# A gated mix of an S4 convolution and a gMLP on one core: the token bias added by VectorE, preparation products taken off GpSimd, idle TensorE work in waits, K products in two groups, and a new order

## The chip, the cores and the metric

The kernel runs on one core of one Trainium2 chip. A core has five engines with instruction streams of their own: TensorE (PE; its weight loads are listed apart as PEld), VectorE (DVE), ScalarE (ACT), GpSimd (POOL) and SyncE (SP), which here only issues DMAs. The metric is the device time of one execution in microseconds, the median of several runs. All operands are bfloat16, accumulation is in float32.

## The reference, cut to what matters

```python
x = A_u                                               # (1, 2048, 640)
g = _sigmoid((x * gate_w).sum(-1, keepdims=True))
a = _A_ref(x, A_re, A_im, B_re, B_im, C_re, C_im, log_dt, Dskip)
b = _B_ref(x, w_in, w_sp, b_sp, w_out)
return g * a + (1 - g) * b

def _A_ref(...):                                      # S4: N = 128 modes per channel
    logdA = dt * A;  dB = dt * Bc
    P = jnp.exp(logdA[:, :, None] * l)                # l = 0 .. 2047
    K = jnp.einsum('dn,dnl,dn->dl', Cc, P, dB).real   # a kernel of 2048 taps per channel
    return irfft(rfft(u padded) * rfft(K padded))[:2048] + u * Dskip

def _B_ref(...):                                      # gMLP, F = 1728, Fh = 864
    z = _gelu(x @ w_in)
    z1 = z[..., :Fh];  z2 = _layernorm(z[..., Fh:])
    g = jnp.einsum('ts,bsf->btf', w_sp, z2) + b_sp[None, :, None]
    return (z1 * g) @ w_out
```

The change touches one term above all: `+ b_sp`, a number for each token t, added to the spatial product before it is multiplied by z1.

## The kernel before, in words

The work is described as tasks, not as a finished program. `add` (L153) notes a task with its engine or a choice of engines, an estimated duration in us, the tiles it reads and writes, and a bias; `dma` (L406) does so for a transfer on a queue of SP or POOL. `Plan.run` (L187) then simulates the engines with these durations, takes for each free engine the ready task with the highest priority (the longest chain behind it, plus its bias), and issues the real instructions in the order found. Where a task names two engines (`("DVE", "ACT")`), the simulation picks one. `TUNE` (L38) adds numbers to the biases, keyed by function, line within the function and a loop index; so the order on every engine is searched offline, and a changed cost or bias moves instructions all over the program. Tiles are taken from rings of a fixed number of buffers (L446); a task that needs a new buffer waits for the last user of the old one.

The stages, in order of time:

- *z2* (`z2_tile`, L587): for each of 16 token tiles ten matmuls of 432 columns (L593), gelu on ACT (L597), a tanh for the gate logit (L599), and sums for the layernorm by DVE (L605) or ACT (L601). A column with gate_w is appended to the weights: it is loaded as `gw5`, transposed on TensorE (L558) and copied by ACT (L560).
- *Preparation* (L728 to L769): products of the S4 parameters on 128 x 640 tiles, by the helpers `ptt` (two tensors, L704), `pts` (scalars, L709), `ftt`/`fts` (with a permuted output, L720/L724) and `pstt`. Most of them may run on DVE or POOL (`pd`). Instructions that these record have the helper's line (L707, L722, L365, L367).
- *z1* (`z1_tile`, L616): 512 tokens by two feature tiles at a time, gelu, and a store to DRAM.
- *Spatial blocks* (`sp_block`, L791): eight blocks of 256 tokens. w_sp arrives transposed (`wT`). For each of seven feature tiles 16 matmuls of 256 columns (L811) accumulate in `ps_g`, two feature tiles to a PSUM tile, and a seventeenth matmul with one contraction row (L813) adds the bias: a row of ones as weights, the bias row `br` (1 x 256) as moving operand. DVE multiplies ps_g by z1 into `vT` (L817, 512 wide; L820, 256 wide on 96 partitions for the last feature tile). Then 28 matmuls with Wout (L834) make `ps_o`, which DVE or ACT scales by 1 - g (L838) into `ob` (stored to DRAM) or, for the last four token tiles, `acc`.
- *K* (`k_exps`, `k_tables`, `k_sub`): in eight steps of 80 channels, exponentials and sines of multiples of the S4 parameters are made by DVE, POOL and ACT into a table ET (two buffers), the multiples among them by `si` (L1003), `ci` and `ai` (L963, L970) and the products by L1019 to L1030. Each step ends in 160 small matmuls (L1047, L1048) in a single task, whose PSUM result goes to `kf` (L1056, L1058) and through DRAM into the layout of the convolution.
- *Convolution*: a factorised Fourier transform, stage 1 of the input (`s1_u`, L640) and of K (`conv_s1`, L1122), the frequency products (`conv_s2`, L1157) with matmuls L1183, L1190, L1198, ACT copies `us` and `vs` and the DVE product `p` (L1192), a DVE transpose (`conv_vt`, L1206), and the inverse (`conv_i2`, L1249) with matmuls L1276/L1278. `i2_out` (L1218) multiplies by g and adds what the gMLP left. The channels are split in a wide part of 480 (h = 0) and a narrow one of 160 (h = 1).

The planned order interleaves the spatial blocks with K and stage 1, so that TensorE has the large products to do while the tables are made.

Of the kernel before, what the change touches and what calls it, by code (L numbers as in the profile page):

```python
# [25 lines left out]
class Handle:  # L26
# [12 lines left out]
    ('conv_s1', 15, ('g', 0)): -4782,  # L39
    ('conv_s2', 35, ('h', 1)): 8481,  # L40
    ('conv_s2', 34, ('h', 0)): 2130,
    ('conv_s2', 34, ('h', 1)): 5372,
    ('conv_s2', 42, ('h', 0)): -1046,
    ('conv_s2', 10, None): 8445,
    ('conv_s2', 14, ('h', 0)): 7450,
    ('conv_s2', 28, None): -242,
    ('conv_vt', 4, ('g', 1)): 16792,
    ('conv_vt', 4, ('g', 2)): 6435,
    ('eights', 6, None): 416,
    ('i2_out', 7, None): -8356,  # L50
    ('k_expand', 28, ('h', 0)): -4317,
    ('k_store', 13, ('h', 0)): 409,
    ('k_sub', 23, None): -4028,
    ('k_sub', 13, ('h', 1)): -5731,
    ('k_tables', 31, ('c', 1)): -9085,
    ('k_tables', 31, None): -2311,
    ('k_tables', 32, None): -5160,
    ('k_tables', 41, ('c', 6)): -7528,
    ('k_tables', 41, None): 3002,
    ('k_tables', 30, None): -7406,  # L60
    ('k_tables', 29, ('c', 2)): -3413,
    ('k_tables', 6, ('c', 2)): 10829,
    ('k_tables', 6, None): -8182,
    ('k_tables', 18, None): 336,
    ('k_tables', 36, ('c', 1)): 8144,
    ('k_tables', 36, None): -161,
    ('k_tables', 20, ('c', 2)): -24903,
    ('k_tables', 20, ('c', 6)): 3906,
    ('k_tables', 20, None): 5307,
    ('k_tables', 21, ('c', 0)): -2613,  # L70
    ('k_tables', 21, ('c', 2)): -28734,
    ('k_tables', 21, None): 7786,
    ('k_tables', 38, ('c', 6)): 11198,
    ('main', 347, None): -1664,
    ('main', 151, ('g', 1)): -2430,
    ('main', 151, ('g', 2)): -4398,
    ('main', 151, ('g', 3)): 29821,
    ('main', 151, None): 1954,
    ('main', 155, None): -1160,
    ('main', 149, None): 906,  # L80
    ('main', 418, None): -10013,
    ('main', 428, None): 7379,
    ('main', 427, None): -8690,
    ('main', 416, None): 58,
    ('quads', 6, None): -16700,
    ('s1_u', 13, ('n0', 2)): 6950,
    ('s1_u', 13, ('n0', 6)): -34683,
    ('s1_u', 16, ('h', 1)): 3532,
    ('s1_u', 16, ('n0', 0)): -364,
    ('s1_u', 16, ('n0', 12)): -37434,  # L90
    ('s1_u', 16, ('n0', 14)): 7826,
    ('s1_u', 16, ('n0', 6)): 3687,
    ('s1_u', 16, None): 3318,
    ('s1_u', 3, ('n0', 12)): 2341,
    ('s1_u', 3, ('n0', 4)): 9125,
    ('s1_u', 18, ('h', 1)): -25774,
    ('s1_u', 18, ('n0', 10)): -2673,
    ('s1_u', 18, ('n0', 4)): -3986,
    ('s1_u', 18, None): -1598,
    ('s1_u', 14, ('h', 1)): -2482,  # L100
    ('s1_u', 14, ('n0', 10)): 4719,
    ('s1_u', 14, ('n0', 4)): -4980,
    ('s1_u', 14, ('n0', 8)): -2369,
    ('s1_u', 14, None): -1332,
    ('sp_block', 28, ('tb', 0)): -5958,
    ('sp_block', 25, ('tb', 6)): 7709,
    ('sp_block', 22, ('tb', 0)): 4394,
    ('sp_block', 22, ('tb', 1)): 1583,
    ('sp_block', 22, ('tb', 6)): -85,
    ('sp_block', 22, ('tb', 7)): 7901,  # L110
    ('sp_block', 44, None): 2232,
    ('sp_block', 45, ('tb', 0)): -19742,
    ('sp_block', 50, ('tb', 2)): -4255,
    ('sp_block', 50, ('tb', 4)): -4889,
    ('sp_block', 50, ('tb', 5)): -664,
    ('sp_block', 50, None): 3599,
    ('sp_block', 3, None): 2228,
    ('sp_block', 8, ('tb', 0)): 27668,
    ('sp_block', 8, None): -3475,
    ('sp_block', 6, None): 11944,  # L120
    ('tg_build', 6, None): 2671,
    ('tg_build', 9, ('c', 0)): 4671,
    ('x_group', 3, ('g', 0)): 2653,
    ('x_group', 3, ('g', 1)): 432,
    ('x_group', 3, ('g', 2)): 3697,
    ('x_group', 3, None): -2901,
    ('z1_tile', 10, ('g', 2)): 850,
    ('z1_tile', 10, None): 4674,
    ('z2_tile', 18, ('h', 0)): -22,
    ('z2_tile', 18, None): -6544,  # L130
# [4 lines left out]
class Plan:  # L135
# [51 lines left out]
    def run(self):  # L187
# [26 lines left out]
        dma = 0.0  # L214
        fset = None
# [7 lines left out]
        while len(order) < N:  # L223
# [10 lines left out]
            while again:  # L234
                again = False
                for e in self.ENG:
# [38 lines left out]
                    for h in t["hs"]:  # L275
                        if h in slot:
                            continue
                        slot[h] = allocs[h.ring]
                        allocs[h.ring] += 1
                        freed[h.ring].append(None)  # L280
                    end = now + max(c - self.OV.get(e, 0.0), 0.03) if c else now
                    if t["nb"]:
                        s = max(end + (0.0 if t["hold"] else 1.0), dma)
                        dma = s + t["nb"] / 1e6
                        fin = dma + (2.5 if t["hold"] else 1.4) + (1.2 if e == "POOL" else 0.0)
                        if t["hold"]:
                            end = dma
                    else:
                        fin = now + c + self.LAT.get(e, 0.0)
# [35 lines left out]
def kernel(  # L325
# [20 lines left out]
    P = 128  # L346
# [57 lines left out]
    QC = {"SP": 0.42, "POOL": 0.6, "ACT": 0.3}  # L404
# [115 lines left out]
    ones = const.tile([1, P], BF, name="ones")  # L520
    vec.memset(ones[:], 1.0)
# [38 lines left out]
    S_(add("ACT", 0.2, lambda e: act.copy(out=Win2[:, :, Fh], in_=psm()[:, 0:ND]), r=[psm], w=["gwt"], bias=9900))  # L560
    add("DVE", 0.3, lambda e: vec.tensor_copy(out=idf[:], in_=ident[:]), r=["pre3"], w=["idf"], bias=1000)
# [142 lines left out]
    def ptt(o, a, b, op, eng=("POOL",)):  # L704
        bf = a in nat or b in nat
# [14 lines left out]
    def ftt(o, a, b, op, eng):  # L720
        cs = [dict(POOL=5.0, DVE=0.3 + dv1(D))[x] for x in eng]
        add(eng, cs, lambda e: parts(e, o, (a, b), lambda o_, i_: E_[e].tensor_tensor(out=o_, in0=i_[0], in1=i_[1], op=op)), r=[a, b, "ptmp"], w=[o], bias=2500)  # L722
# [69 lines left out]
    def sp_block(tb):  # L792
# [6 lines left out]
        br = sbt(lambda: gsp, "br", "br", [1, 256])  # L799
        dma("SP", lambda: br()[:], lambda: brv[:, 256 * tb:256 * tb + 256], 512, r=["br_d"], w=[br], bias=1000 - 100 * tb)  # L800
        vT = []
        for f0 in range(0, NFT, 2):
            ps = gps("ps_g", [P, 2, 256])
            fts = range(f0, min(NFT, f0 + 2))
            for ft in fts:
                fs = fsz[ft]

                for c0 in range(0, NS, 4):
                    def m(e, ft=ft, fs=fs, ps=ps, f0=f0, c0=c0):
                        for st in range(c0, c0 + 4):  # L810
                            pe.matmul(ps()[0:fs, ft - f0, :], lhsT=z2n[:, st, 128 * ft:128 * ft + fs], rhs=wT()[:, st, :], start=(st == 0), stop=False)  # L811
                        if c0 + 4 == NS:
                            pe.matmul(ps()[0:fs, ft - f0, :], lhsT=ones[0:1, 0:fs], rhs=br()[:], start=False, stop=True)  # L813
                    add("PE", (4 + (c0 + 4 == NS)) * mm(256), m, r=([(wT, 0), (wT, 1), br] if c0 == 0 else [wT, br]) + ([(ps, f0)] if ft > f0 and c0 == 0 else []) + [("z2n", s) for s in range(c0, c0 + 4)], w=[(ps, ft)], bias=-1000 - 100 * tb)
            v_ = sbt(lambda: gsp, "vT", "vT", [P, 2, 256], bufs=4)
            if f0 < 6:
# [552 lines left out]
```

## Time and profile before

| | us |
|---|---|
| median of 5 runs | 362.28 (360.02 to 363.6) |
| the profiled execution | 363.6 |
| its span | 361.8 |
| TensorE busy (mean granted clock 0.973) | 325.2 |
| VectorE busy | 280.1 |
| ScalarE busy | 239.3 |
| GpSimd busy | 155.5 |
| 896 spatial matmuls L811, busy | 113.1 |
| 32 + 16 products p (L1192), busy | 47.9 |

Busy time of TensorE counts each matmul from its start to a modelled end, and successive matmuls overlap: 896 x 276 ns would be 247 us, yet the group's busy time is 113.1. What a matmul takes from its engine is therefore read from the starts of its neighbours in the timeline. The clock of TensorE is not constant; the profile gives the granted share for each stretch. A line of the profile's list of groups names the line in the code, the engine, the operation, the written and read tiles, the shape, the count, then the busy time and the mean of one in ns, and after the last bar the idle time of the engine just before them and what ended it. A line of waits reads "engine, tile and line that waited <- engine, tile and line that it waited for: us in total, times, the longest".

### The profile page before, as it was taken

The page shows a single profiled execution, that of the slowest core. Times are in us where ns is not written, and L with a number is a line of the kernel's source. Part 1 is how long each engine was busy: PE and PEld are TensorE (multiplying, and loading weights), DVE is VectorE, ACT ScalarE, POOL GpSimd, SP SyncE. Part 2 cuts the span into 40 slices and gives each one's busy share as a digit, 9 for nine tenths or more (in the row PEclk, how much of TensorE's full clock was granted, in tenths as well). Part 3 has the DMA queues.
Part 4 walks back from the last instruction along what each step waited for, and adds up shares of the span by engine and source line. Part 5 has one row for each costly group of instructions (what it writes and reads, how often), then busy time and mean ns, then how long its engine had stood idle before and what let it go on. Part 6 is the DMA issues. An engine that isn't in the chain of part 4 may idle for free. (4 is left out here: it accounts for less than half of the span.)

```text
span 361.8 us, 8375 instructions
## 1 busy us (share of the span) xinstructions
PE 325.2 (90%) x3225; PEld 214.2 (59%) x3225; DVE 280.1 (77%) x520; ACT 239.3 (66%) x429; POOL 155.5 (43%) x168
## 2 busy tenths in 40 slices
PE   0899988999999999979998998999999999969854
PEld 0355544777776767766775576767763333558631
DVE  4029999698788559995497869867579788899985
ACT  1685854899795467686976773755449888606742
POOL 3025424710089307974087859646477002100241
PEclk9999999999999989997999999999999999998996
DMA  7968998369384339486645347899938766582216
GB/s 204 195 123 147 218 242 285 88 145 224 82 213 153 98 83 250 49 189 94 189 121 125 96 67 185 213 247 270 274 129 209 212 170 201 154 245 67 73 56 181
DMA packets 106361, 59.37 MB, mean 164 GB/s; under 512 B 74586, under 2 KB 102714, under 8 KB 106322
## 3 DMA queue, kind: packets, MB, share of 16 engines
q1 hardware_dynamic: 104034, 54.00, 59.3%
q0 software_dynamic: 2288, 4.85, 5.8%
q8 instruction: 25, 0.41, 0.5%
q14 instruction: 14, 0.11, 0.1%
HBM read 24.73 MB, written 19.47 MB: 122 GB/s over the span
## 5 line engine op out<-in xcount | busy, mean ns | idle before, releaser
L811 PE MATMUL ps_g<-wT,z2n 128*128 128x256 bf16 (+1 forms) x896 | 113.1, 276 | 1.2 <-DVE vT L817 0.7
L811 PEld LDWEIGHTS <-z2n 128*128 128x128 bf16 (+1 forms) x896 | 87.2, 102 | 21.6 <-issue 3.2
L1192 DVE TENSOR_TENSOR p<-ps_s2k,us 128x960 bf16<-128x960 f32 (+1 forms) x48 | 47.9, 1037 | 8.4 <-ACT us L426 5.4
L365 POOL TENSOR_SCALAR si<-th 128x80 int32<-128x80 f32 x56 | 45.3, 809 | 7.5 <-DVE ci L365 1.8
L365 POOL TENSOR_SCALAR ci<-ai 128x640 int32<-128x640 int32 (+1 forms) x11 | 21.8, 1990 | 55.7 <-ACT ET L419 28.2
L625 PE MATMUL ps_z<-xg,Win 128*128 128x512 bf16 (+1 forms) x140 | 33.5, 387 | 4.4 <-ACT zt L419 2.6
L1200 ACT CAST vs<-ps_v 128x480 bf16<-128x480 f32 (+1 forms) x48 | 24.9, 524 | 14.6 <-PE ps_v L1198 14.3
L834 PE MATMUL ps_o<-Wout,vT 128*128 128x320 bf16 (+1 forms) x224 | 33.7, 299 | 0.0
L593 PE MATMUL ps_z<-Win,xT 128*128 128x432 bf16 (+1 forms) x160 | 32.4, 363 | 1.1 <-ACT gl L599 1.0
L1047 PE MATMUL ps_k<-ET 128*32 128x33 bf16 x640 | 28.3, 259 | 3.1 <-DVE ET L1021 1.6
L419 ACT ACTIVATE ET<-ci 128x640 bf16<-128x640 int16 (+1 forms) x40 | 26.3, 676 | 6.2 <-POOL ci L365 3.1
L1047 PEld LDWEIGHTS <-ET 128*32 128x32 bf16 x640 | 27.0, 193 | 4.9 <-DVE ET L1021 2.2
L1190 PE MATMUL ps_s2k<-fk,T 128*128 128x480 bf16 (+1 forms) x128 | 24.1, 305 | 5.3 <-DVE p L1192 4.9
L1048 PE MATMUL ps_k<-ET 128*32 128x33 bf16 x640 | 28.1, 258 | 0.0
L1048 PEld LDWEIGHTS <-ET 128*32 128x32 bf16 x640 | 27.5, 195 | 0.7 <-issue 0.7
L426 ACT CAST us<-ps_u 128x480 bf16<-128x480 f32 (+1 forms) x48 | 24.5, 525 | 5.0 <-PE ps_u L1183 4.1
L834 PEld LDWEIGHTS <-vT 128*128 128x128 bf16 (+1 forms) x224 | 21.6, 98 | 9.2 <-issue 0.2
L1198 PE MATMUL ps_v<-p,G 128*128 128x480 bf16 (+1 forms) x128 | 25.7, 307 | 1.0 <-ACT us L426 0.2
L593 PEld LDWEIGHTS <-xT 128*128 128x128 bf16 x160 | 16.0, 101 | 16.5 <-issue 3.9
L625 PEld LDWEIGHTS <-Win 128*128 128x128 bf16 (+1 forms) x140 | 14.0, 103 | 19.8 <-issue 6.0
L419 ACT ACTIVATE mr<-lre 128x320 bf16<-128x320 f32 x66 | 24.9, 455 | 0.0
L414 POOL DMA_DIRECT2D FK_d<-s1k x9 | 7.6, 846 | 39.7 <-ACT s1k L426 34.0
(193 smaller groups left out, 618.0 us busy)
## 6 DMA issues: line engine op xcount, KB each, us to landing
FU_d<-s1u SPq DMA_DIRECT2D x16, 240.0 KB
fu<-FU_d SPq DMA_DIRECT2D x16, 240.0 KB
fk<-FK_d SPq DMA_DIRECT2D x16, 240.0 KB
z_d<-zt SPq DMA_DIRECT2D x24, 128.0 KB
z1t<-z_d SPq DMA_DIRECT2D x8, 384.0 KB
xf<-in_A_u_dram SPq DMA_DIRECT2D x8, 320.0 KB
FK_d<-s1k POOLq DMA_DIRECT2D x5, 480.0 KB, 6.4
Win<-in_B_w_in_dram SPq DMA_DIRECT2D x2, 1080.0 KB
```

What stands on the lines that cost most here:

```text
L365: eng.tensor_scalar(out=out_, in0=in_, scalar1=s1, scalar2=None, op0=op0)
L419: return add("ACT", cost, lambda e: act.activation(out=out_(), in_=in_(), func=func, scale=scale), r=r, w=w, fset=fs, bias=bias, deps=deps ...
L426: (vec.tensor_copy if e == "DVE" else act.copy)(out=out_(), in_=in_())
L593: pe.matmul(ps()[:, h, 0:432 + h], lhsT=xT[:, i, 128 * st:128 * st + 128], rhs=Win2[:, i, 432 * h:432 * h + 432 + h], start=(i == 0), stop ...
L625: pe.matmul(ps()[0:fs, ft - f0, :], lhsT=Win1[:, i, 128 * ft:128 * ft + fs], rhs=xg()[:, i, :], start=(i == 0), stop=(i == ND - 1))
L811: pe.matmul(ps()[0:fs, ft - f0, :], lhsT=z2n[:, st, 128 * ft:128 * ft + fs], rhs=wT()[:, st, :], start=(st == 0), stop=False)
L834: pe.matmul(ps()[:], lhsT=vT[ft // 2]()[0:fs, ft % 2, 128 * r:128 * r + 128], rhs=Wout[0:fs, ft, HD * h:HD * h + HD], start=(ft == 0), sto ...
L1047: pe.matmul(o_, lhsT=ET[:, 0:32, d], rhs=M2[:, :, d], start=True, stop=False, tile_position=(0, 32 * q))
L1048: pe.matmul(o_, lhsT=ET[:, NA:NA + 32, d], rhs=E2[:, :, d], start=False, stop=True, tile_position=(0, 32 * q))
L1192: add("DVE", dv1(2 * NW), lambda e, p12=p12, ps=ps, us=us: vec.tensor_tensor(out=p12()[:, :, 0:NW], in0=ps()[:, :, 0:NW], in1=us()[:, 0:NW ...
L1198: pe.matmul(pv()[:, W * n:W * n + W], lhsT=GV(k + n, i), rhs=p12()[:, i, W * n:W * n + W], start=(i == 0), stop=(i == 1))
L1200: add("ACT", 0.15 + NW / 1170, lambda e, k=k, pv=pv: act.copy(out=X["vs"][h][:, k:k + NK, :], in_=pv()[:, 0:NW].rearrange("p (k d) -> p k ...
```

## The change

- `sp_block`: the seventeenth matmul and the `ones` tile go. `br` becomes 128 x 256, the bias row broadcast to all partitions by its load on SP (eight loads of 64 KB in place of 0.5 KB). DVE first adds ps_g and br into vT, then multiplies vT by z1 in place: 32 more DVE instructions, 24 of 128 x 512 and 8 of 96 x 256.
- `ptt` and `ftt`: the engine is DVE whatever the call says. Two products for Wr and Wi, lnW, lre, and two smaller ones that the old order had on POOL move to DVE; in the new order phi, ax and a scaling of t move to POOL.
- `k_sub`: one task of 160 matmuls becomes two of 80, the second planned at least 1.3 us after the first, with ready work of other kinds between.
- Idle TensorE work: 32 transposes of the identity ahead of the first z2 tile (their results are not used), and matmuls of 256 columns in the tail, 12 (h = 0) and 24 (h = 1), whose results are overwritten.
- The planner's costs: half clock for 3.2 us after a TensorE pause of over 2.1 us, shorter DMA latencies, longer DMA issues and POOL steps; and a new `TUNE`, so that the order on all engines differs. Among the moves: on SP, ldt is issued ahead of the second half of w_in and gw5, and the six parameter loads (nat) ahead of all loads xg; on ACT the exponential of ldt stands ahead of the copy of the gate column. Evacuations change engines: of the stage-1 copies of 320 columns DVE has 11 instead of 5, of the kf copies 3 instead of 6, of ob 12 instead of 16 and of acc 5 instead of 2; POOL makes 48 si rows instead of 56.

The lines of `TUNE` (some 90 numbers) are left out:

```diff
-    ones = const.tile([1, P], BF, name="ones")
-    vec.memset(ones[:], 1.0)
...
+    def warm0(e):
+        for k in range(4):
+            pe.transpose(out=psm()[:, 256 + 128 * k:384 + 128 * k], in_=ident[:], identity=ident[:])
+    for k in range(8):
+        add("PE", 4 * mm(128), warm0, r=["pre3"], w=[(psm, "w")], bias=-9000)
...
     def ptt(o, a, b, op, eng=("POOL",)):
+        eng = ("DVE",)
...
     def ftt(o, a, b, op, eng):
+        eng = ("DVE",)
...
-        br = sbt(lambda: gsp, "br", "br", [1, 256])
-        dma("SP", lambda: br()[:], lambda: brv[:, 256 * tb:256 * tb + 256], 512, r=["br_d"], w=[br], bias=1000 - 100 * tb)
+        br = sbt(lambda: gsp, "br", "br", [P, 256])
+        dma("SP", lambda: br()[:], lambda: brv[:, 256 * tb:256 * tb + 256].to_broadcast([P, 256]), 65536, r=["br_d"], w=[br], bias=1000 - 100 * tb, run=512)
...
-                            pe.matmul(ps()[0:fs, ft - f0, :], lhsT=z2n[:, st, 128 * ft:128 * ft + fs], rhs=wT()[:, st, :], start=(st == 0), stop=False)
-                        if c0 + 4 == NS:
-                            pe.matmul(ps()[0:fs, ft - f0, :], lhsT=ones[0:1, 0:fs], rhs=br()[:], start=False, stop=True)
+                            pe.matmul(ps()[0:fs, ft - f0, :], lhsT=z2n[:, st, 128 * ft:128 * ft + fs], rhs=wT()[:, st, :], start=(st == 0), stop=(st == NS - 1))
...
-                add("DVE", dv1(512), lambda e, v_=v_, ps=ps, f0=f0: vec.tensor_tensor(out=v_()[:], in0=ps()[:], in1=z1t()[:, f0:f0 + 2, :], op=ALU.mult),
-                    r=[(ps, f) for f in fts] + [(z1t, 0)], w=[v_], bias=9500)
...
+            nf, pb = len(fts), fsz[f0]
+            add("DVE", dv1(256 * nf), lambda e, v_=v_, ps=ps, nf=nf, pb=pb: vec.tensor_tensor(out=v_()[0:pb, 0:nf, :], in0=ps()[0:pb, 0:nf, :], in1=br()[0:pb, :].unsqueeze(1).to_broadcast([pb, nf, 256]), op=ALU.add),
+                r=[(ps, f) for f in fts] + [br], w=[(v_, "g")], bias=9500)
+            add("DVE", dv2(256 * nf), lambda e, v_=v_, f0=f0, nf=nf, pb=pb: vec.tensor_tensor(out=v_()[0:pb, 0:nf, :], in0=v_()[0:pb, 0:nf, :], in1=z1t()[0:pb, f0:f0 + nf, :], op=ALU.mult),
+                r=[(v_, "g"), (z1t, f0 // 6)], w=[v_], bias=9000)
...
-        def m(e):
+        def m(e, hf):
             ET, M2, E2 = X["ET", z], X["M2", z], X["E2", z]
-            for i in range(SQ):
+            for i in range(SQ // 2 * hf, SQ // 2 * hf + SQ // 2):
...
-        tab_ids.append(add("PE", 3.65, m, r=tabs + (["cva"] if h else []), w=[ps], bias=8000, lag=[(tab_ids[-1], 4.0)] if tab_ids else []))
+        for hf in range(2):
+            tab_ids.append(add("PE", 1.85, lambda e, hf=hf: m(e, hf), r=tabs + (["cva"] if h else []), w=[(ps, hf)], bias=8000 + 500 * hf, lag=[(tab_ids[-1], 1.3 if hf else 4.0)] if tab_ids else []))
...
+            if u == 0:
+                def warm(e, pj=pj):
+                    for k in range(4):
+                        pe.matmul(pj(0)[:, 0:256], lhsT=HT[:, 0, :], rhs=Wout[:, k, 0:256], start=True, stop=True)
+                for k in range((3, 6)[h]):
+                    add("PE", 4 * mm(256), warm, r=["HT", "Wout0"], w=[pr[0]], bias=-9000, deps=[mv_id[h]])
```

## The prediction, written before the changed kernel ran

> **What bounds the kernel now.** I read the page first (which engine is busy), then the stretches between the stages, then the order of the instructions on TensorE, then who waits for whom.
>
> ```profile
> PE 325.2 (90%) x3225; PEld 214.2 (59%) x3225; DVE 280.1 (77%) x520; ACT 239.3 (66%) x429; POOL 155.5 (43%) x168
> ```
>
> TensorE is the fullest engine, but 90% is an average. The table of stretches cuts the span where the limit changes: z2 until 43.08, the parameter work until 62.30, the long middle with w_sp, Wout, the K tables and stage 1 until 267.75, the frequency products of the wide half until 313.94, and the tail.
>
> ```profile
> 0.00:43.08 43.08, 32.96 (x164) 16.53 (x165) 22.49 (x75) 25.14 (x55) 14.76 (x24) 1.00 0.82 177
> 43.08:62.30 19.22, 16.97 (x89) 8.61 (x88) 19.22 (x46) 10.75 (x17) 6.36 (x6) 1.00 0.94 252
> 62.30:267.75 205.45, 197.81 (x2495) 144.90 (x2493) 158.90 (x306) 143.89 (x234) 112.85 (x112) 0.98 0.65 158
> 267.75:313.94 46.19, 43.24 (x200) 18.91 (x198) 38.27 (x40) 38.50 (x74) 13.44 (x20) 1.00 0.66 181
> 313.94:361.80 47.86, 34.21 (x284) 25.23 (x282) 41.20 (x58) 21.00 (x52) 8.06 (x9) 0.90 0.42 127
> ```
>
> The first two numbers after the interval are its length and TensorE's busy time, then weight load, DVE, ACT, GpSimd. In the second stretch DVE is full (19.22 of 19.22). In the third TensorE is (197.81 of 205.45), with DVE 46.5 us idle. In the last DVE leads. So a TensorE saving counts in the third stretch and hardly elsewhere.
>
> What one bias matmul costs there is read from starts, not from busy time:
>
> ```profile
> 69.57 0.57 PE L652 MATMUL ps_s<-xf,F 128*128 128x480 bf16 x2
> 69.97 1.91 PE L811 MATMUL ps_g<-wT,z2n 128*128 128x256 bf16 x16
> 71.82 0.28 PE L813 MATMUL ps_g<-br,ones 1*128 1x256 bf16 x1
> 72.03 2.68 PE L811 MATMUL ps_g<-wT,z2n 128*128 128x256 bf16 x23
> ```
>
> Sixteen L811 matmuls take 1.85 us from 69.97 to 71.82. At the ordinary spacing of 0.109 us the bias matmul would start 15 x 0.109 + 0.109 = 1.74 after the first and its successor 0.109 later. Instead the start is 0.1 late, and the successor waits 0.21: together 0.205 + 0.21 - 0.109 = 0.307 us for one matmul with a single row of weights. The weight loader's waits name the same place:
>
> ```profile
> PEld L813 <- issue: 11.0, 53, 0.2
> ```
>
> 53 of the 56 lie in the third stretch, each with a 0.2 us pause before its weights. DVE's own waits there:
>
> ```profile
> DVE kf L1056 <- PE ps_k L1048: 11.9, 4, 4.2
> DVE vT L817 <- PE ps_g L813: 8.2, 6, 2.8
> DVE s1u L426 <- PE ps_s L652: 6.7, 4, 2.8
> DVE ob L365 <- PE ps_o L834: 3.8, 6, 1.9
> ```
>
> Some 31 of DVE's 46.5 idle us wait for TensorE, so they are room for more DVE work.
>
> **The change, part by part.**
>
> *Bias matmuls removed.* 53 x 0.307 = 16.3 us of TensorE time in the third stretch. The other three stand at 316 to 321 us, under eight DVE transposes of 9.43 us: nothing.
>
> *Bias as a DVE add, then a multiplication.* The add has the form of the old operation (a PSUM tile with an SBUF tile) and its price, so it costs nothing new. The multiplication is new and reads two SBUF tiles. Nearest rows:
>
> ```profile
> L817 DVE TENSOR_TENSOR vT<-ps_g,z1t 128x512 bf16<-128x512 f32 x24 | 16.1, 682 | 8.4 <-PE ps_g L813 8.2
> ...
> L1233 DVE TENSOR_TENSOR wT<-tm,wT 128x480 bf16<-128x480 bf16 x2 | 0.8, 408 | 1.0 <-ACT tm L1231 1.0
> ...
> L1233 DVE TENSOR_TENSOR wT<-tm,wT 128x160 bf16<-128x160 bf16 x4 | 0.8, 231 | 0.0
> ```
>
> 0.41 us for the wide tiles and 0.27 (between the two L1233 rows) for the narrow: 21 x 0.41 + 7 x 0.27 = 10.5 us in the third stretch. Next to GpSimd such an operation is slower in places:
>
> ```profile
> 120.53 0.81 DVE L1020 TENSOR_TENSOR ET<-ET,mr 128x1280 bf16<-128x1280 bf16 x1
> ...
> 138.53 1.33 DVE L1020 TENSOR_TENSOR ET<-ET,mr 128x1280 bf16<-128x1280 bf16 x1
> ```
>
> Bounds: 10.5, and 1.33 / 0.81 of it, 17.2. The five L1020 that ran wholly beside GpSimd work average 1.02, a quarter more, and GpSimd is busy 55% of the stretch (112.85 of 205.45): 1.14 x 10.5 = 12.0 us, which I take. The Trainium skill speaks against this part: "Advanced Engine Details and Errata", section "VectorE Performance Modes", says that the second SBUF port of VectorE is shared with GpSimd and that the two interfere. The rows agree in part, 1.33 against 0.81. By a full block of the one while the other runs, the multiplications would cost up to 17 us and the forecast would rise by some 3 us.
>
> The multiplication sits in the chain from ps_g to ps_o and makes vT 0.41 us later; behind it on DVE wait table steps and evacuations; four vT tiles cover it. Its PSUM tile is freed by the add, as before.
>
> *br broadcast:* eight loads of 64 KB in place of 0.5 KB, the same number of issues on SP, 0.5 MB of 59 MB with DMA 65% busy: 0, at most 8 x 0.4 us (64 KB at 158 GB/s) if all were exposed.
>
> *Preparation products off GpSimd.* DVE is full here, so this moves the second stretch. Three DVE operations beside a GpSimd product took 1.71, 1.50 and 1.28 instead of 0.81, and six z2n steps at 57.43 took 4.87, against 6 x 0.43 alone: 4.3 us of slowing that can go. Six products at 0.81 to 0.88 come in, some 5 us, of which about 0.8 falls behind 62 us. That cancels. phi, ax and the scaled t go the other way, onto GpSimd at some 2.1 to 2.4 us each, where more time leaves (1.40, 1.40, 2.12, 2.37 and two of some 1.4). The parameter loads are issued on SP ahead of all xg loads, so part of the 2.31 us that DVE idles ahead of 25.50 can go. I take -1.5, bounds -3 and +1.
>
> *Idle work at the start.* 32 transposes ahead of z2. The two at L780 took 0.46 us together, 0.11 to 0.23 each, so 3.5 to 7.4 us from about 6.2 us on, ending at 9.7 to 13.6; z2 began at 9.60:
>
> ```profile
> 9.44 0.18 PE L558 MATMUL pt_s<-ident,gw 5*128 5x5 bf16 x1 [3.23 <-DMA gw<-in_gate_w_dram]
> 9.60 3.77 PE L593 MATMUL ps_z<-Win,xT 128*128 128x432 bf16 x10
> ...
> 13.50 2.46 PE L593 MATMUL ps_z<-Win,xT 128*128 128x432 bf16 x10
> ```
>
> Later groups of ten take 1.86, so warming is worth up to 1.9 + 0.6 = 2.5 us and the transposes can delay by up to 4. But z1 starts at 43.08 when Win1 has landed (issued at 36.58, and about there after the change), so an earlier z2 gains 0.5 at most. On SP, ldt moves ahead of Win2 and gw (0.36 us to issue, 160 KB or 0.9 us at 177 GB/s, so z2 may start 1 us later), and on ACT its Exp with a table load (1.28 + 0.74) moves ahead of the copy of the gate column, out of the way of the first z2 evacuations, which cost TensorE 1.04 us at 16 us. I take 0 for the start, bounds -0.5 and +3. The Trainium skill has a rule against the transposes: "TensorE: Matmul & The Clock Gate", "Part 4: PE-mode transpose", says that transposes do not count as busy for the clock gate. No row here shows it. By it the start would come out up to 3 us later instead of unchanged.
>
> *K products in two groups.* The clock falls after some of them:
>
> ```profile
> 160.00:170.00 10.00, 9.21 (x155) 6.78 (x147) 7.18 (x13) 7.43 (x15) 4.47 (x7) 0.66 0.72 112
> ```
>
> Records at double spacing run from 127.09 to 130.5 and from 161.22 to 168.05, a loss of 1.7 + 3.4 = 5.1 us. Only two of eight products are followed by one, so whether the split cures them is open: gain 0 to 5.1, I take 0. The second group comes 1.3 us or more later, which delays kf's evacuation; the other ET buffer covers it.
>
> *Warm matmuls in the tail.* 24 of 256 columns, 24 x 0.109 = 2.6 us, in waits of 3.70 us (352.30): 0, bounds -0.5 and +2.
>
> *The order of the third stretch.* TensorE needs 205.45 - 7.6 (gaps) - 5.1 (half clock) - 16.3 = 176.4. DVE: 158.9 + 12.0 + about 4.0 of parameter work that slides in + s1u 6 x 0.48, s1k 1.2, table steps 1.6, less kf 3 x 0.99, gb 0.7 and ob/acc 0.5 = 176.4. Both have the same load. TensorE with its old gaps and half clocks gives 189.1; DVE with its old 15.5 us of waits for others than TensorE gives 191.9. Two engines both over 90% full disturb one another, so I take 194: -11.5.
>
> *The wide frequency products* are bound by the alternation of ACT and DVE, 4.16 us for three: 0, -2 to +2. *The tail:* two p's and two vT operations (2 x 0.77 and about 1.0 us on DVE) move ahead of the transposes; I take -2, -4 to +2.
>
> Sum: -11.5 - 1.5 - 2 = -15 against the profiled execution's 363.6 (span 361.8): 348.6. That execution is 1.3 above the median of 362.28, so 347.
>
> **The rivals.**
>
> *DVE becomes the bound, slower than before.* The K tables now end just ahead of their products (slack 0 to 0.4 us at 122.5, 146.2, 158.9 and 191.2). If the added operations push them back, DVE keeps its old idle time instead of filling it. With 40 of the 46.5 us kept the stretch is 176.4 + 40 = 216.4, +11; less 3.5 elsewhere +7.5, so 370. The point is 32.5 us kept for no change, 36 for 1% slower. For it: the zero slack. Against it: 31 us of that idle is waiting for TensorE, which gets faster.
>
> *The same, milder.* 28 to 30 us kept: stretch 205, no gain there: 359.
>
> *The bias matmul was cheap.* If only its streaming of 0.109 us is saved and the pause falls to another boundary: 53 x 0.109 = 5.8 us, TensorE with gaps 199.6, -5.8 - 3.5: 353. Against it: ps_o's 28 matmuls and the ps_g series show no pause at their own boundaries.
>
> *DVE keeps up and the half clock goes.* Stretch 187 (-18.5), with the rest -22: 340.
>
> **How the numbers follow.** Forecast 0.53, cheap bias matmul 0.13, all goes well 0.13, milder DVE bound 0.09, DVE bound and slower 0.12. The likeliest case alone runs from 342 to 352. The range reaches to the neighbours: 339 to 359; outside are the slower case and the ends of two others. About 1% is what a measurement can tell from no change; that is below 358.7 or above 365.9. Faster: 0.53 + 0.13 + 0.13 = 0.79; within 1%: 0.09; slower: 0.12.
>
> **What the profile after would show.** Right: a middle stretch of about 194 us with TensorE and DVE both near 177 of it, the multiplication at 0.41 to 0.5 us, ps_g groups following one another without the 0.2 us pause. Wrong: DVE waits for TensorE turning into TensorE waits for ET, vT or kf; z2 starting after 12 us; GpSimd steps stretching DVE; the multiplication near 0.68, which adds 8 us to DVE's load.

## The result, and the profile after

The changed kernel takes 366.94 us (median of 25 runs) where the kernel before takes 361.76 (median of 46): a ratio of 1.012, 95% interval 1.0096 to 1.0143, so it is slower by 1.2%. The medians in this text are of all executions of a kernel, the ratios of its fast executions alone (those within 1.5% of its fastest, here 16 of 26), so the two need not agree. The forecast was 347, and 359 the upper end of the range. The profiled execution below took 368.39 (span 366.6), 1.5 above the median.

The engines of the changed kernel, then its stretches, cut at the same events as before (start of z1, first spatial product, first frequency product, first transpose of the tail):

```profile
PE 316.3 (86%) x3237; PEld 220.4 (60%) x3237; DVE 288.3 (79%) x559; ACT 240.8 (66%) x429; POOL 146.8 (40%) x161
```

```profile
0.00:46.38 46.38, 36.60 (x197) 19.90 (x197) 25.74 (x92) 27.20 (x58) 8.62 (x19) 1.00 0.85 171
46.38:66.00 19.62, 19.34 (x109) 10.64 (x107) 17.85 (x44) 11.09 (x15) 9.44 (x7) 1.00 0.89 216
66.00:272.67 206.67, 185.39 (x2451) 144.44 (x2449) 166.15 (x329) 145.00 (x236) 108.64 (x110) 0.98 0.70 161
272.67:321.07 48.40, 46.39 (x252) 23.90 (x250) 40.20 (x45) 38.41 (x75) 12.63 (x19) 1.00 0.78 230
321.07:366.60 45.53, 28.63 (x238) 21.56 (x236) 38.37 (x55) 19.09 (x47) 7.42 (x8) 0.88 0.24 73
```

Against before the five lengths differ by +3.3, +0.4, +1.2, +2.2 and -2.3, in all +4.8 us of span. The third line is the one to look at: TensorE is busy 12.4 us less (185.39 against 197.81), as the change intends, and the stretch is no shorter. The time has become idle time, 21.3 us in place of 7.6. TensorE's waits in that stretch of the changed kernel say for what:

```profile
PE ps_g L808 <- DVE vT L812: 10.6, 10, 1.7
PE ps_u L1178 <- DMA fu<-FU_d: 4.8, 1, 4.8
```

(total us, times, longest). The first was 0.7 us in all before; the second is new. TensorE now stands more often before a buffer that DVE has not emptied yet, and a load comes late. Whether the added DVE work makes these waits is tested below. At the start, TensorE of the changed kernel reads:

```profile
5.99 3.62 PE L553 MATMUL pt_s<-ident 128*128 128x128 bf16 x32
12.33 0.18 PE L548 MATMUL pt_s<-ident,gw 5*128 5x5 bf16 x1 [2.73 <-DMA gw<-in_gate_w_dram]
12.45 3.79 PE L588 MATMUL ps_z<-Win,xT 128*128 128x432 bf16 x10
```

The gate column lands 2.9 us later than before (12.33 against 9.44), behind ldt on SP. TensorE idles 2.73 us after the warming transposes, and the first ten z2 matmuls take 3.79 us, as long as before without the transposes (3.77).

### The profile page after: what moved, and what is told of

Read it like the earlier page. It is cut to its first block, busy times and chain, and to the rows that moved or that the text cites. A ratio compares the mean times of both kernels' runs of the same rounds, so it can differ in the third digit from the quotient of the medians.

```text
span 366.6 us, 8425 instructions
## 1 busy us (share of the span) xinstructions
PE 316.3 (86%) x3237; PEld 220.4 (60%) x3237; DVE 288.3 (79%) x559; ACT 240.8 (66%) x429; POOL 146.8 (40%) x161
## 4 chain that ended last, share of the span: by engine, by line
PE 37%; SPq 18%; DVE 17%; ACT 12%; DMA 9%; issue 4%; POOL 2%; DVEq 0%; ACTq 0%
SPq L404 15%; PE ps_g L808 12%; ACT mr L411 5%; PE ps_z L620 4%; DMA xk<-KA_d 4%; PE ps_o L828 4%; PE ps_s2k L1185 4%; DVE vs L1201 4%; SPq L406 3%; PE ps_v L1193 3%; DVE p L1187 3%; DMA fu<-FU_d 2%; PE ps_k L1041 2%; PE ps_k L1042 2%; PE ps_u L1178 2%
## 5 line engine op out<-in xcount | busy, mean ns | idle before, releaser
L808 PE MATMUL ps_g<-wT,z2n 128*128 128x256 bf16 (+1 forms) x896 | 110.0, 276 | 10.9 <-DVE vT L812 10.6
L808 PEld LDWEIGHTS <-z2n 128*128 128x128 bf16 (+1 forms) x896 | 90.1, 103 | 29.4 <-issue 13.3
L357 POOL TENSOR_SCALAR si<-th 128x80 int32<-128x80 f32 x48 | 41.7, 869 | 10.1 <-DVE ci L357 4.2
L357 POOL TENSOR_SCALAR ci<-ai 128x640 int32<-128x640 int32 (+1 forms) x8 | 15.0, 1877 | 48.4 <-ACT s1u L418 26.0
L620 PE MATMUL ps_z<-xg,Win 128*128 128x512 bf16 (+1 forms) x140 | 31.8, 379 | 0.0
L1041 PE MATMUL ps_k<-ET 128*32 128x33 bf16 x640 | 29.1, 260 | 1.4 <-DVE ET L1024 1.4
L1042 PE MATMUL ps_k<-ET 128*32 128x33 bf16 x640 | 28.7, 258 | 0.0
L588 PEld LDWEIGHTS <-xT 128*128 128x128 bf16 x160 | 16.1, 102 | 16.8 <-issue 4.4
L418 ACT CAST s1k<-ps_s1k 128x960 bf16<-128x960 f32 (+1 forms) x18 | 15.2, 848 | 16.7 <-PE ps_s1k L1131 10.2
L1185 PEld LDWEIGHTS <-T 128*128 128x128 bf16 x128 | 11.9, 102 | 19.0 <-issue 13.8
```

The source lines that it names most:

```text
L357: eng.tensor_scalar(out=out_, in0=in_, scalar1=s1, scalar2=None, op0=op0)
L418: (vec.tensor_copy if e == "DVE" else act.copy)(out=out_(), in_=in_())
L588: pe.matmul(ps()[:, h, 0:432 + h], lhsT=xT[:, i, 128 * st:128 * st + 128], rhs=Win2[:, i, 432 * h:432 * h + 432 + h], start=(i == 0), stop ...
L620: pe.matmul(ps()[0:fs, ft - f0, :], lhsT=Win1[:, i, 128 * ft:128 * ft + fs], rhs=xg()[:, i, :], start=(i == 0), stop=(i == ND - 1))
L1041: pe.matmul(o_, lhsT=ET[:, 0:32, d], rhs=M2[:, :, d], start=True, stop=False, tile_position=(0, 32 * q))
L1042: pe.matmul(o_, lhsT=ET[:, NA:NA + 32, d], rhs=E2[:, :, d], start=False, stop=True, tile_position=(0, 32 * q))
```

## The experiments

Each keeps the order of instructions of the kernel that it starts from, apart from the lines named. A ratio is to the kernel before on the same chip. The first four change the bias alone.

**The bias moved in the kernel before, nothing else.**

```diff
-  pe.matmul(..., lhsT=ones[0:1, 0:fs], rhs=br()[:], start=False, stop=True)
-  v_ = ps * z1t
+  v_ = ps + br
+  v_ = v_ * z1t
```

> The kernel before in its own order, with only the bias moved: no bias matmuls, br broadcast, DVE adds and then multiplies at the place where it multiplied. Theory A (VectorE takes it back: the saved TensorE time returns as TensorE waits for ps_g to be freed, because the second DVE instruction lengthens the in-order queue): within 3 us of before. Theory B (the move is worth what was forecast, and the new order loses it): 10 us or more below before, some 350. Theory C (TensorE's time was never the limit of the middle; the K tables and the transfers behind them are): 0 to 4 us below before, with longer TensorE idle time that does not wait for DVE's vT.

365.87 us, 1.0113 (1.0074 to 1.0152). The move alone, in the old order, loses as much as the whole change. Its middle stretch:

```profile
62.30:267.90 205.60, 181.68 (x2437) 142.61 (x2438) 167.39 (x332) 143.91 (x233) 114.49 (x111) 0.98 0.66 161
```

It is as long as before (205.45), with TensorE 16.1 us less busy: the freed time has become idle time, as in the change, without any new order.

**The bias matmuls left out of the kernel before.**

```diff
-  pe.matmul(..., lhsT=ones[0:1, 0:fs], rhs=br()[:], start=False, stop=True)
```

> The kernel before in its own order with the 56 bias matmuls left out and nothing in their place (b_sp is not added). It prices the matmuls without any DVE work. A and B: 10 to 16 us below before, 346 to 352. C: 0 to 4 us below before, about 359.

358.91 us, 0.993 (0.9903 to 0.9957). The step that was to bring 16.3 us brings 2.4 (1.6 to 3.5 by the interval), although no other engine gets more to do.

```profile
62.30:262.11 199.81, 182.48 (x2437) 143.58 (x2437) 157.66 (x305) 143.53 (x233) 112.44 (x111) 0.97 0.68 161
```

In this one execution TensorE's busy time falls by 15.3 us, its idle time grows from 7.6 to 17.3. Next to the run before (1.0113 / 0.993), the add and the multiplication cost 1.8%, some 6.6 us, for 9.7 us more DVE busy time in the stretch (167.39 against 157.66). The prediction had hidden all of it. What TensorE waited for, in the kernel before, in the run with the bias moved and in this one:

```profile
PE ps_g L811 <- DVE vT L817: 0.7, 2, 0.4
PE ps_g L811 <- DVE vT L817: 4.4, 6, 1.3
PE ps_g L811 <- DVE vT L817: 3.8, 6, 1.3
```

So nearly all of the growth of this wait is there without any added DVE work: TensorE is done sooner and waits for the same DVE queue. The cost of the moved bias appears elsewhere. The last K product begins at 238.6 us with the bias moved and at 235.6 without it (242.0 before), and the stretch after it takes 29.4 us against 26.6. The wider load of `br` is no rival: the kernel before with full-height weights, below, has it too and is faster.

**The multiplication left out of the changed kernel; the bias put back on TensorE there.**

```diff
-  v_ = v_ * z1t                                      # the first
+  pe.matmul(..., lhsT=ones[0:1, 0:fs], ...)          # the second
+  v_ = ps * z1t
```

> The changed kernel in its order, with the 32 added multiplications left out (z1 is not multiplied in); the add stays. A: 8 to 10 us below the changed kernel, near 357, and the waits of ps_g for vT shrink from 10.6 us to under 4. B: no more than 2 us below it. C: 0 to 3 us below it.

> The changed kernel in its order, with the bias put back on TensorE (56 matmuls of one row) and a single DVE multiplication. A: 0 to +4 us against the changed kernel, 366 to 371, the waits of ps_g for vT falling by about as much as the matmuls cost. B: +12 to +16, about 380. C: 0 to +4, with no change in the transfers around 220 to 250 us.

The first: 367.0 us, 1.0144 (1.0101 to 1.0186), no faster than the changed kernel (1.012). The second: 370.9, 1.0245 (1.0205 to 1.0286), slower than it by 4 us. The group of ps_g matmuls in the changed kernel, then in these two runs (the last number is its wait for vT):

```profile
L808 PE MATMUL ps_g<-wT,z2n 128*128 128x256 bf16 (+1 forms) x896 | 110.0, 276 | 10.9 <-DVE vT L812 10.6
L808 PE MATMUL ps_g<-wT,z2n 128*128 128x256 bf16 (+1 forms) x896 | 107.8, 273 | 11.2 <-DVE vT L812 11.2
L808 PE MATMUL ps_g<-wT,z2n 128*128 128x256 bf16 (+1 forms) x896 | 114.2, 275 | 4.6 <-DVE vT L812 3.3
```

Without the multiplications the wait is as long as with them; it shrinks when TensorE has the bias matmuls to do. So here too the wait comes from TensorE's being early rather than from DVE's second instruction. Theory A falls with this, and B with the run before it. C fits the times of these three runs, but not that of the first, in which the moved bias cost time.

So in the new order VectorE's multiplication is covered, and the bias move is a gain of 1.2% by itself; in the old order it is a loss of 1.1%. That leaves about 2.4% (the second run, with the work of before) to be lost by the new order and the other edits.

**Large cuts in the kernel before: is TensorE the bound of the middle, or VectorE?** The first leaves out the bias and half of the spatial matmuls, the second three of the table multiplications on DVE, the third those and the bias, the fourth also some of the ACT exponentials of the tables, the fifth is the first two together.

```diff
-  pe.matmul(ps, lhsT=z2n[:, st, ...], rhs=wT[:, st, :], ...)
+  if st % 2 == 0 or st == 15: pe.matmul(...)         # half g
...
-  vec.tensor_tensor(out=E2, ...); ... out=M2 ...; ... out=E1 ...   # L1019, L1021, L1030
+  None                                               # light tables
```

> Without the 56 bias matmuls the kernel before gained only 2.4 us, so TensorE's time is not the price it seemed. This run finds the floor: the kernel before in its order, 9 of 16 ps_g matmuls kept in each group and no bias matmuls (the rest of the spatial sum and b_sp are left out), some 60 us of TensorE work less. If other chains (tables, transfers) set the end of the middle: 3 to 10 us below before, 352 to 358, with TensorE idle for the rest. If TensorE is the limit once the order allows it: 25 us or more below, under 337.

354.33 us, 0.9811 (0.9743 to 0.9879). Its middle stretch and the longest of TensorE's waits there:

```profile
62.00:256.50 194.50, 150.97 (x2072) 109.53 (x2073) 155.68 (x302) 142.28 (x233) 112.94 (x110) 0.92 0.66 165
```

```profile
PE ps_g L811 <- DVE vT L817: 12.9, 9, 3.5
PE ps_k L1047 <- DVE ET L1030: 5.6, 3, 4.1
PE ps_k L1047 <- DVE ET L1021: 4.8, 2, 4.3
```

Seven of sixteen matmuls of the largest product are gone, TensorE is busy 46.8 us less in this stretch (not 60: its mean clock there was 0.92 instead of 0.98, so what was left took longer) and the kernel gains 7.9 by the medians, 1.9% by the ratio. TensorE now waits for vT and for the tables.

> The kernel before in its order, with three of the four products of sines and exponentials left out of each K table (L1019, L1021, L1030: 33 us of DVE; the tables lack these factors), all TensorE work kept. If DVE's chain to the tables limits the middle: 10 us or more below before, 351 or less. If TensorE limits it: 0 to 3 below. If transfers limit it: 0 to 4 below.

355.51 us, 0.9834 (0.9773 to 0.9894): 33 us of VectorE work off, 6.7 gained. So VectorE's load alone isn't the bound either.

> As the run before it (three table products left out), and the 56 bias matmuls left out too (no b_sp). If DVE and TensorE limit the middle in turn, so that each alone gains little: the matmuls now bring 8 to 16 us on top of the run with light tables. If a third chain (transfers, ACT) limits it: again only 2 to 4 us on top.

352.88 us, 0.9762 (0.9674 to 0.985): with room on VectorE the bias matmuls are still worth only 2.6 us.

> The run with three table products and the bias matmuls left out (352.9), with 16 of the 33 narrow exponentials of each of the two sets left out as well (32 ACT instructions of 0.456 us; the tables lack them). If ACT's exponentials set the first and the fifth K product, each comes some 7 us earlier and the time falls by 8 to 14 us, to 339 to 345. If TensorE or transfers hold it then: 0 to 4 us.

The four executions took 353.83, 353.19, 353.11 and 347.49 us, beside a median of 352.88 without that cut. Three show no gain and one 5 us, and there is no ratio; the 8 to 14 us of the first theory did not come. The first K product began 1.5 us earlier (104.2 against 105.7), not 7. TensorE was nearly full in the steps up to it (42.01 of 43.00 us), so this says nothing of ACT where TensorE is not.

> The kernel before in its order with both cuts at once: 9 of 16 ps_g matmuls kept and no bias matmuls (some 60 us of TensorE), and three of four table products left out (33 us of DVE). Alone they brought 7.7 and 6.7 us. If TensorE and DVE hold the middle in turn, so that each cut runs into the other engine: together clearly more than the sum of 14, 20 to 35 us, to 327 to 342. If a third chain holds it (transfers, ACT, the tail of the span): no more than the sum, 347 to 355.

345.09 us, 0.956 (0.9518 to 0.9602): 16 us, about the sum of the two cuts (14.6).

```profile
62.00:247.40 185.40, 148.60 (x2081) 108.78 (x2080) 126.34 (x279) 141.95 (x233) 93.34 (x110) 0.94 0.73 174
```

With 49 us of TensorE's busy time and 33 of VectorE's away, the stretch shrinks by 20 and no engine is busy more than 81% of it. So it is not the sum of either engine's work that holds it. What does, the chain of a table step through the engines, ScalarE, or the transfers, stays open; a further run, with the exponentials left out on top of these cuts, gave no result. All these runs leave work out of an order that was planned with it. What a plan made for the lighter work would gain was not tried.

**The parts of the change undone in the changed kernel.** ldt's load issued after the gate column's; no idle work; each K product in one piece; the preparation products back on GpSimd:

```diff
-  ldt, gw5        # order of the loads on SP
+  gw5, ldt
...
-  for k in range(4): pe.transpose(...) / pe.matmul(...)    # warm0, warm
+  for k in range(0): ...
...
-  for i in range(SQ // 2 * hf, SQ // 2 * hf + SQ // 2):
+  for i in range(SQ if hf == 0 else 0):
...
-  vec.tensor_tensor(out=Wr, ...)     # also Wi, t2, t3, lre, lnW
+  pool.tensor_tensor(...)
```

> The changed kernel with one swap on SP: gw5 is issued ahead of ldt again (still behind the second half of w_in). z2 began at 12.45 us instead of 9.60 after waiting for gw5. If this transfer's place makes the late start and the start is carried to the end: z2 begins near 10 us, and the time falls by 2 to 3 us against the changed kernel's 366.9. If the start is absorbed later (first K product only 1.5 us late): 0 to 1 us.

364.38 us, 1.0063 (1.0025 to 1.0102). z2 begins at 10.0 instead of 12.45 and z1 at 43.4 instead of 46.4, and about half of the loss of 1.2% goes.

> The changed kernel with its idle TensorE work left out: the 32 transposes ahead of z2 and the 36 matmuls in the tail. Theory D (the end is set by a chain of steps with different limits; TensorE's work in the middle fills gaps, and the changed kernel loses at the ends of the chain): the 20 matmuls ahead of the third-last group took 3.3 us at the half clock and the last groups queued behind them, so the time falls by 2 to 3 us against the changed kernel, to 364 or 365; the start does not move, since z2 waits for gw5. Rival: the idle work pays for itself by the clock, and the time rises by 1 to 2 us.

367.48 us, 1.0166 (1.012 to 1.0211): overlaps the changed kernel's interval. No gain or loss by the idle work can be measured, so theory D's 2 to 3 us are not there; the gate column is used from 11.97 without it (12.33 with it), so the transposes don't delay z2 by more than 0.4 us.

> The changed kernel with the K products in one group of 160 again, at the place of the first half. Theory D: the same within 1.5 us, since a K step waits for its tables. Rival (the split is what keeps the clock up and it matters): half-clock stretches after K products return, and the time rises by 2 to 5 us.

375.13 us, 1.0368 (1.0319 to 1.0417): 2.5% slower than with the split, which neither side expected. TensorE waits 15.3 us for vT in place of 10.6, and VectorE 13.7 us for stage 1 in place of 7.0; the mean clock is below 1 in the same neighbourhoods in both (0.83 from 150 to 160 us in either, 0.66 from 248 to 258 with the split and 0.83 from 246 to 256 without). That points to the other work that the split lets in between. A part of the clock isn't excluded: over the whole span it averaged 0.962 in these four executions and 0.974 in the 26 of the changed kernel. The order was made for two pieces, so it isn't the price of the split in general.

> The changed kernel with Wr, Wi, lnW, lre and the two small products back on GpSimd at the same places. Theory D: the exponentials on ACT set the first K product, and these products are needed early, so it is slower by 0 to 3 us, with the first K product up to 3 us later. Rival (they are hidden, as the forecast of -1.5 with an upper bound of +1 would allow): within 1 us.

367.85 us, 1.0141 (1.0082 to 1.0201): no difference from the changed kernel (1.012) that can be measured. The interval leaves room for the forecast of -1.5 and for nothing.

**The late load.** In the changed kernel SP issues, and TensorE waits:

```profile
238.16 5.40 SPq L404 DMA_TRANSPOSE wT<-in_B_w_sp_dram  x1
243.66 3.63 SPq L406 DMA_DIRECT2D fu<-FU_d  x3
```

```profile
251.69 0.56 PE L1178 MATMUL ps_u<-fu,T 128*128 128x480 bf16 x1 [4.83 <-DMA fu<-FU_d]
```

One transposing load occupies SP for 5.40 us while the DMA engines are full (their share from 218 to 252 us is 1.03), and three fu loads queue behind it. This run issues it after them:

```diff
-  wT (tb 7, r 1), fu (h 0; k = 0, 2, 4)    # on SP
+  fu (h 0; k = 0, 2, 4), wT (tb 7, r 1)
```

> The changed kernel with one transposed load of w_sp (second half of the last block) moved behind three loads of fu on SP; in the changed kernel it held SP for 5.4 us at 238 and TensorE then waited 4.8 us for fu. If this transfer's place is what delays the first frequency products (272.7 against 267.8 before): they start 3 to 5 us earlier and the time falls by 2 to 5 us. If the transfers as a whole are full there (DMA share 1.03 from 218 to 252): 0 to 1 us, and something else waits.

366.33 us, 1.0063 (1.0019 to 1.0107). The ratio rests on five of twelve executions, which spread from 360.6 to 369.8; the median of all is only 0.6 below the changed kernel's, so a gain is not sure. The frequency products begin at 271.9 instead of 272.7, not 3 to 5 us earlier. The wait for fu is gone, and the next one took most of its place:

```profile
258.18 1.76 PE L1131 MATMUL ps_s1k<-xk,F 128*128 128x480 bf16 x4 [3.88 <-ACT s1k L418]
```

With the gate column's move as well:

> The changed kernel with both transfer moves of the runs above: gw5 ahead of ldt, and one transposed load of w_sp behind three loads of fu. Each alone brought about 2 us. If the two losses stand in one chain one after the other: 4 us below the changed kernel, 362 to 363, the same as before. If they share a cover: 364 to 365.

365.59 us, 1.008 (1.0048 to 1.0113). Together about 0.4%, no more than the gate column's move alone, and less than either theory gave them.

**The bias matmul with full-height weights.** Weights of 128 rows of 1/128 in place of one row of 1, and br on all 128 partitions, first in the kernel before, then in the changed one in place of the DVE add:

```diff
-  ones = const.tile([1, P]);  vec.memset(ones, 1.0)
-  pe.matmul(..., lhsT=ones[0:1, 0:fs], rhs=br()[:], ...)       # br (1, 256)
+  ones = const.tile([P, P]);  vec.memset(ones, 1.0 / 128.0)
+  pe.matmul(..., lhsT=ones[:, 0:fs], rhs=br()[:], ...)         # br (P, 256)
```

> The kernel before in its order, with the bias matmul kept on TensorE but given 128 contraction rows: weights of 1/128 everywhere, the bias row broadcast to 128 partitions by its load. If the 0.2 us pause belongs to weights of one row, it goes, each bias matmul costs the ordinary 0.109 us, and of the 2.4 us that leaving them out brought 1 to 2 us are won: 359.5 to 360.5. Rival (the pause belongs to the end of the group): the pauses stay and the time is that of before.

357.86 us, 0.9869 (0.9841 to 0.9897): faster than both kernels, with all of the computation, and below the 359.5 to 360.5 expected. The same place of its trace as the prediction showed:

```profile
69.20 1.91 PE L811 MATMUL ps_g<-wT,z2n 128*128 128x256 bf16 x16
70.95 0.27 PE L813 MATMUL ps_g<-br,ones 128*128 128x256 bf16 x1
71.06 3.22 PE L811 MATMUL ps_g<-wT,z2n 128*128 128x256 bf16 x28
```

The bias matmul starts 1.75 after the first of its sixteen (1.85 before) and its successor 0.11 later (0.21 before): the late start and the pause are gone. So they belong to the single row and not to the end of the group.

> The changed kernel in its order with the bias back on TensorE in the form without a pause (128 rows of 1/128), and a single DVE multiplication. With one-row weights it was at 370.9, with the DVE add and multiplication at 366.9. By the 4.2 us that this form brought in the order of before: 366 to 367, so the new order is some 8 us slower than the old one at equal work. Rival (the new order has a use for both savings): 362 or less.

367.99 us, 1.0222 (1.0171 to 1.0272). In the new order the form is worth 0.2% by the ratios and 0.8% by the medians against one-row weights (1.0245, 370.9), not the 1.3% of the old order. With the same bias on TensorE in both, the new order with the other edits is 3.6% slower than the old one by the ratios (1.0222 / 0.9869), 3.1% by the medians, each against the kernel before on its chip.

## Why the prediction was wrong, point by point

**The step that failed** is "So a TensorE saving counts in the third stretch and hardly elsewhere", and with it the term "Bias matmuls removed. 53 x 0.307 = 16.3 us". The price of one matmul was about right: the successor starts 0.2 us sooner once the weights have 128 rows. But leaving all of them out gains 2.4 us, and leaving out seven of sixteen spatial matmuls as well gains 7.9. TensorE at 197.81 of 205.45 looked like a bound, but its in-order queue holds spatial matmuls between all table steps. They fill time that the steps need anyway; shortened, they leave a wait. The steps between the K products of the kernel before show that the limit changes hands inside the stretch:

```profile
62.30:109.20 46.90, 46.87 (x366) 34.60 (x363) 39.41 (x82) 41.87 (x72) 16.34 (x19) 1.00 0.63 154
109.20:122.50 13.30, 13.30 (x218) 8.87 (x217) 11.65 (x24) 8.17 (x12) 11.37 (x12) 1.00 0.41 129
146.20:158.90 12.70, 11.02 (x217) 8.95 (x217) 12.17 (x21) 9.51 (x17) 12.18 (x12) 1.00 0.38 98
232.10:267.75 35.65, 34.84 (x530) 26.41 (x530) 23.22 (x45) 18.18 (x24) 19.98 (x22) 1.00 0.97 252
```

TensorE is nearly full in most of them, but not by need: with seven of sixteen spatial matmuls gone, the first K product still began at 107.3 instead of 109.2. In the first row ScalarE is at 41.87 of 46.90; in the second VectorE and GpSimd are at 11.65 and 11.37 of 13.30, in the third nearly full (12.17 and 12.18 of 12.70); in the last the DMA engines are (0.97). The mean over 205 us, 158.9 for DVE and 143.9 for ACT, hides this. That each of these sets its step is read from busy shares; no run took them away one by one.

**VectorE's waiting as room.** "Some 31 of DVE's 46.5 idle us wait for TensorE, so they are room for more DVE work" failed in the old order (6.6 us lost for 9.7 of work) and held in the new for the multiplication (no gain by leaving it out). Room counts only at the place where the work lands. In the old order half of what the DVE work cost had arisen by the last K product (3.0 us) and half after it (2.8 us), in the profiled executions; TensorE's waits for vT grew by 0.6. Which DVE step passes the delay on was not followed.

**Sizes.** The multiplications were sized nearly right. In the changed kernel:

```profile
L814 DVE TENSOR_TENSOR vT<-vT,z1t 128x512 bf16<-128x512 bf16 x24 | 10.0, 443 | 0.0
L814 DVE TENSOR_TENSOR vT<-vT,z1t 96x256 bf16<-96x256 bf16 x8 | 2.8, 347 | 0.1
```

In the third stretch they are busy 10.9 us beside the forecast 12.0, though the trace holds 29 there, not the 28 counted. Single ones reach 0.84 us. The section that the prediction cites for such slowing (the Trainium skill, "Advanced Engine Details and Errata", "VectorE Performance Modes") names two-port instructions of VectorE, and its table gives a product of two tensors no two-port mode, so it says less of this case than the prediction took from it. That GpSimd causes the slowing is not shown here either: three of the five L1020 that ran wholly beside GpSimd took 0.81 us. The third stretch came out at 206.67 beside 194; the others: preparation +0.4 beside -1.5 (inside its bounds), frequency products +2.2 beside 0 (just past the upper bound of 2), tail -2.3 beside -2.

**The start** was taken as 0 with an upper bound of +3. z2 began 2.85 late, mostly for the reason given (ldt ahead of the gate column on SP, priced there at 1 us; moving it back took 2.4 off), and z1 began 3.3 late. "So an earlier z2 gains 0.5 at most" says nothing of a later one: here the lateness reached z1 in full.

**The rivals.** The time came out on the side of "DVE becomes the bound, slower than before" (370), which had 0.12; so it was right in its direction and not for its reason. In the changed kernel its mechanism did not come: the first pieces of the K products start at 110.7 to 234.9 us where the whole ones started at 109.2 to 242.0, so the last table is 7 us earlier. The time is lost after it: the first wide frequency product starts at 272.67 instead of 267.75. From the last K product to there, before and after:

```profile
242.00:267.75 25.75, 25.75 (x332) 19.59 (x332) 14.92 (x30) 11.75 (x15) 14.74 (x17) 1.00 0.93 244
234.90:272.67 37.77, 32.60 (x366) 25.08 (x366) 23.36 (x44) 14.17 (x16) 18.90 (x21) 0.91 0.91 218
```

TensorE is busy 6.9 us longer there and idle 5.2. The second bias run, which has the work of before, shows the same: 34.4 us with TensorE busy 32.3, the first frequency product 7.1 later than before and the profiled execution 7.3 longer. All runs in the new order need 34 to 41 us from the last K product to the first frequency product, those in the old order with all spatial matmuls and tables 24 to 29. So the new order leaves more of TensorE's work behind the last K product. The prediction had no term for this. It is read from the profiles; no run moved the work back.

**What stays open.** Of the new order's loss the runs place about half a per cent (the gate column's load; the move of the w_sp load adds nothing sure). The profiles show the rest behind the last K product, but it lies in no single part that was undone: idle work and preparation are worth nothing measurable, and undoing the split makes it worse. What holds the middle stretch with both engines lightened is open too.

## What to carry to other kernels

Price a saving on a busy in-order engine by leaving the work out in the same order, before the change is built: some 60 us of TensorE work left out brought 7.9, while its busy share was 96%. Cut a long stretch at the events that pace it (here the K products) and read each piece; a share near 100% over the whole may be filler between steps that other engines set. And look first for a cheaper form on the same engine: the bias on full-height weights moved no work to another queue and was the only version here that beat both kernels with all of the computation.

## What the runs showed of the hardware

A matmul with one contraction row among matmuls with 128 rows took some 0.31 us of TensorE's time here, with 128 rows 0.12 by the same count (1.75 + 0.11 - 16 x 0.109). The cheap form gained 1.3%, more than leaving the matmul out (0.7%, intervals 0.9841 to 0.9897 and 0.9903 to 0.9957); why is not settled. The granted clock differs in the same direction: over the span it averaged 0.967 in the ten executions without the matmuls, 0.978 in the six with the cheap form, and 0.975 to 0.977 in the kernel before beside them.

Transposes on TensorE went along with a fast start when only pauses of about 1 us followed. In the run with both load moves:

```profile
5.99 3.62 PE L553 MATMUL pt_s<-ident 128*128 128x128 bf16 x32
...
11.39 1.82 PE L588 MATMUL ps_z<-Win,xT 128*128 128x433 bf16 x9 [1.01 <-ACT Win L550]
```

Nine matmuls take 1.82 us here, at full speed (the run with the gate column's move alone has the same), where ten took 3.79 in the changed kernel after a pause of 2.73 us, 3.79 in it without transposes, and 3.77 in the kernel before. The rule that the prediction weighed against them (the Trainium skill, "TensorE: Matmul & The Clock Gate", Part 4: transposes don't count as busy for the clock) is not what these rows show. That the pause behind them took the benefit away in the changed kernel fits the rows; it was not tested by itself.
